# Lasting row tiles, set-up work dealt over the slots, experts that begin three slots later, and fewer scatters between the last blocks

## The chip, the cores and the metric

The kernel runs on one core of a Trainium2 chip. The metric is the device time of one execution in microseconds; less is better. Before the change it is 595.44 us (median of three runs, 592.53 to 595.68).

## What is computed

The input is x, 8 batches of 2496 tokens with 256 features. A filter over each batch's sequence comes first, then a mixture of 8 experts of which each token uses one:

```
X = rfft(x, axis=1);  y = irfft(X * (filt_r + 1j*filt_i), n=2496, axis=1)
x = y.reshape(19968, 256)
logits = x @ w_gate + modality_bias[modality_id]          # 19968 x 8
e = argmax(logits);  gate = max(softmax(logits))
out = gate * (relu(x @ w1[e]) @ w2[e])                    # w1: 256x1024, w2: 1024x256
```

## The kernel before, in words

The transform of length 2496 is written as 48 by 52. Stage 1 multiplies by the 48 part, stage 2 by the 52 part, filters and turns back by 52, stage 3 turns back by 48 and leaves the rows of tokens. Between the stages the data are laid out anew: for batches 0 to 2 on the chip by TensorE transposes (`turned1`, `to_residues`, `to_columns`), for batches 3 to 7 through DRAM (`load_t2`, `load_t4`, on SP's queue). Stage 2 is cut into 12 pieces of two frequencies; `around` runs the forward products of one piece and the inverse ones of the piece ahead of it, with something from another batch between them. One such step, and whatever stands beside it, is a slot here. In the trace the two forward products at L474 open a slot.

Stage 3 has 10 steps of two row groups each. A batch's rows stand in a row tile: 128 partitions, 20 row groups, 130 words each, that is 128 words with the row in 16 bits, one with the token's number (`DW`) and one with its gate. The row tile comes from a pool `yp` of two buffers. At step 0 GpSimd writes the token numbers (L555, the token add) behind the last TensorE mark (`paced`); VectorE and ScalarE write the rows in turn (L599, L597). Each step also transposes rows (L584) and adds up the logits (L589).

After stage 3 a batch is routed: `counting` finds each row's expert and its rank within it, `placing` makes the positions in the experts' bins, `scatter` (L677) writes one row group into the bins in DRAM by an indirect DMA from GpSimd, 20 per batch, and `tabling` finds which expert blocks are full. `pace(k)` issues at most one scatter per call and returns what is left of k, so nested calls issue several.

`Experts` then runs blocks of 256 rows: SP loads the block from the bins (`xs`, L755), TensorE transposes it (L784), multiplies by w1 (L798), by w2 (L811), and two indirect DMAs from GpSimd write the scaled rows to their tokens (L820). One call of `moe.step` is a quarter of a block's products. The weights come during the first stretches by `load_w` on GpSimd's queue, as x does by `load_x`.

The program has five parts, and within them the order on TensorE, ScalarE and VectorE is the order in which the code is written (`manual_schedule`) in the stretches ahead of the merged loop:

- Set-up: the constants of the transform are made, and batch 0's stage 1 runs beside.
- First stretch, `spectrum(0, ...)`: 13 slots with batch 0's stage 2, and more constants at four places between slots; `busy(3)` issues three spare products per slot.
- Second stretch, `both(1, k)`: 15 slots with batch 1's stage 2 and batch 0's stage 3. Third, `both(2, k)`: 15 slots with batch 2's and batch 1's; here batch 0 is routed (`some` takes pieces of it per slot) and scattered.
- Merged loop, n from 0 on: stage 2 and 3 of the later batches, two or three scatters per slot, and 1.5 expert steps per slot. The first blocks of experts start `LAG` slots behind the slot they are given.
- Tail: beyond n = `end` each turn of the loop issues `pace(1)` and one whole block, until batch 7's scatters are out; then blocks alone. Seventy-nine blocks run in all.

Each engine works through its own queue in order. On SP's queue, stage 2's loads of batch 3 stand among the loads of expert blocks; on GpSimd's, token adds stand among scatters, stores of expert rows and loads of x and of weights.

## Time and profile before

| what | value |
|---|---|
| median of three runs | 595.44 us |
| profiled execution, its own time | 595.62 us |
| its span, first to last instruction | 593.4 us |
| mean granted TensorE clock | 0.944 of full speed |
| TensorE products busy | 511.0 us, 86 % |
| VectorE, ScalarE, GpSimd busy | 372.5, 380.4 and 371.5 us |
| scatters (L677) | 160, 164.5 us |
| stores of expert rows (L820) | 158, 161.7 us |

Set-up ends near 25 us; the first stretch runs from 24.8 to about 54, the second from 55 to 79, the third from 81 to about 118, the merged loop begins behind it, the tail at about 397, and blocks run alone from 482.5. Busy time is an average over parts with different limits. The timeline shows each instruction's start, duration and, in brackets, how long its engine had idled and for whom; the windows view gives the engines' busy time in a stretch; the chain of waits goes back from the last instruction. A granted clock near 0.5 is the lower of TensorE's two levels (1.2 GHz of 2.4), and L474's pair then takes 0.63 us in place of 0.38.

### The profile page before, as it was taken

Reading aid. Unit: us, or ns where it says so; the run is one execution under the profiler, and the core shown is the slowest. Engines: PE = TensorE matmul, PEld = TensorE weight load, DVE = VectorE, ACT = ScalarE, POOL = GpSimd, SP = SyncE. Lnnn points to the kernel's source line nnn. Section 1 sums busy time; section 2 is a strip of 40 time slices with the busy share of each in tenths; the row PEclk is TensorE's granted clock in tenths of the full one; section 3 lists DMA queues with packets and bytes.
Section 4 is the critical chain, followed back from the end, with each engine's and each line's share of the span. In section 5 each row is a group of like instructions: output and inputs, shape, how many; then the busy total and the mean of one; then the engine's idle time right before and its main releaser. Section 6 shows DMA issues by size and latency. Waiting matters only on the chain.

```text
span 593.4 us, 16261 instructions
## 1 busy us (share of the span) xinstructions
PE 511.0 (86%) x5115; PEld 461.3 (78%) x5115; DVE 372.5 (63%) x1207; ACT 380.4 (64%) x695; POOL 371.5 (63%) x409
## 2 busy tenths in 40 slices
PE   2678978749988996999898997998999999999990
PEld 2567968638867896988887995986888889999990
DVE  8556978646657677677778785784455365555540
ACT  4677968727847786787786772554656556666660
POOL 8123315737756775676776777777777776555552
PEclk9979998959988999899999997998999999999996
DMA  8999994788498878889758545334433344333220
GB/s 152 177 159 206 211 213 101 175 185 215 127 225 226 226 161 217 227 187 246 225 151 229 158 134 161 95 94 145 140 112 117 118 124 135 109 106 110 93 72 23
DMA packets 69301, 93.29 MB, mean 157 GB/s; under 512 B 11427, under 2 KB 52841, under 8 KB 69059
## 3 DMA queue, kind: packets, MB, share of 16 engines
q0 software_dynamic: 21504, 50.75, 35.0%
q1 hardware_dynamic: 24409, 29.94, 19.7%
q10 hardware_dynamic: 23302, 11.50, 7.5%
q8 instruction: 48, 0.79, 0.6%
q14 instruction: 38, 0.31, 0.2%
HBM read 64.68 MB, written 46.35 MB: 187 GB/s over the span
## 4 chain that ended last, share of the span: by engine, by line
PE 45%; DMA 15%; issue 15%; DVE 10%; POOL 9%; ACT 3%; DVEq 1%; POOLq 0%; SPq 0%; ACTq 0%
PE hps L798 12%; PE ops L811 11%; POOL out_dram L820 7%; DMA out_dram<-osb,meta 5%; DMA t<-b_d 3%; PE ps L474 3%; PE lt L584 3%; PE ps L569 2%; DMA bins_d<-yo,pos_i 2%; PE pz L486 2%; PE pz L487 2%; DMA b_d<-t 2%; PE ps L572 2%; DVE osb L818 2%; PE pT L784 1%
## 5 line engine op out<-in xcount | busy, mean ns | idle before, releaser
L803 ACT ACTIVATE hT<-hps 128x512 f16<-128x512 f32 x316 | 188.3, 598 | 117.2 <-PE hps L798 116.3
L820 POOL DMA_INDIRECT out_dram<-osb,meta x158 | 161.7, 1024 | 80.9 <-DVE osb L818 35.2
L798 PE MATMUL hps<-xT,w 128*128 128x256 f16 x1264 | 201.7, 280 | 5.1 <-DVE xT L785 4.7
L677 POOL DMA_INDIRECT bins_d<-yo,pos_i x160 | 164.5, 1028 | 57.3 <-issue 21.8
L811 PE MATMUL ops<-w2sb,hT 128*128 x1264 | 196.8, 276 | 3.2 <-issue 2.4
L798 PEld LDWEIGHTS <-w 128*128 128x128 f16 x1264 | 147.0, 147 | 12.1 <-DVE xT L785 7.6
L811 PEld LDWEIGHTS <-hT 128*128 128x128 f16 x1264 | 124.9, 99 | 19.6 <-issue 4.2
L818 DVE TENSOR_SCALAR osb<-ops,meta 128x256 f32<-128x256 f32 x158 | 69.5, 477 | 43.1 <-DMA out_dram<-osb,meta 25.7
L776 DVE COPY w<-w1sb 128x2048 f16 x79 | 55.6, 704 | 29.0 <-PE hps L798 27.1
L508 DVE TENSOR_TENSOR p<-xf,g 104x512 f16<-104x512 f16 x96 | 40.5, 421 | 45.3 <-ACT xf L501 45.0
L501 ACT CAST xf<-ps 104x512 f16<-104x512 f32 x96 | 57.3, 597 | 7.8 <-PE ps L474 6.9
L785 DVE COPY xT<-pT 128x512 f16<-128x512 f16 x79 | 33.4, 423 | 41.8 <-PE pT L784 40.8
L523 ACT CAST z<-pz 104x512 f16<-104x512 f32 x72 | 42.9, 596 | 13.1 <-PE pz L487 9.5
L474 PE MATMUL ps<-t,w2m 104*104 104x256 f16 x192 | 39.7, 290 | 7.4 <-DMA t<-b_d 4.5
L219 ACT CAST t<-ps 96x512 f16<-96x512 f32 x52 | 30.2, 581 | 24.0 <-PE ps L215 21.1
L509 DVE TENSOR_TENSOR xf<-xf,g 104x512 f16<-104x512 f16 x96 | 40.5, 422 | 3.0 <-DVE p L508 0.3
L144 POOL DMA_DIRECT2D xt<-in_x_dram x32 | 18.2, 571 | 35.6 <-PE fp L215 13.7
L784 PE MATMUL pT<-ident,xs 128*128 128x128 f16 x316 | 31.5, 223 | 10.1 <-DMA xs<-bins_d 9.5
L486 PE MATMUL pz<-p,a1m 104*104 104x256 f16 x144 | 37.2, 281 | 3.4 <-DVE p L508 1.9
L593 DVE COPY yT<-lt 128x512 f16<-128x512 f16 x80 | 33.4, 418 | 7.1 <-PE lt L589 5.1
L487 PE MATMUL pz<-xf,a2m 104*104 104x256 f16 x144 | 36.6, 279 | 0.0
L584 PE MATMUL lt<-ident,yo 128*128 128x128 f16 x320 | 31.0, 218 | 5.9 <-DVE yo L599 3.2
(206 smaller groups left out, 723.7 us busy)
## 6 DMA issues: line engine op xcount, KB each, us to landing
xs<-bins_d SPq DMA_DIRECT2D x79, 130.0 KB
xt<-in_x_dram POOLq DMA_DIRECT2D x24, 384.0 KB
t<-b_d SPq DMA_DIRECT2D x18, 384.0 KB
t<-b_d SPq DMA_DIRECT2D x15, 416.0 KB
b_d<-z ACTq DMA_DIRECT2D x30, 208.0 KB
b_d<-t ACTq DMA_DIRECT2D x24, 192.0 KB
w1sb<-in_moe_w_dram POOLq DMA_DIRECT2D x16, 256.0 KB
w2sb<-in_moe_w_dram POOLq DMA_DIRECT2D x8, 512.0 KB
```

The source lines that it names most:

```text
L474: mm = nc.tensor.matmul(ps[:KB, i, :], lhsT=w2m[:, s + i, :], rhs=st[g]["t2", s // SCH][:, s % SCH + i, :], start=True, stop=True)
L486: nc.tensor.matmul(pz[:KB, i, :], lhsT=a1m[:, s + i, :], rhs=p1[:, i, :], start=True, stop=False)
L487: nc.tensor.matmul(pz[:KB, i, :], lhsT=a2m[:, s + i, :], rhs=p2[:, i, :], start=False, stop=True)
L501: nc.scalar.copy(xf, ps[:KB])
L584: nc.tensor.transpose(pT[:, i, dc, :], yo[:, ub + i, dc * P:(dc + 1) * P], ident)
L677: ins = nc.gpsimd.indirect_dma_start(out=bins_d[:, :], out_offset=IOA(ap=st[g]["pos"][:rows, t:t + 1], axis=0), in_=st[g]["yw"][:rows, t, ...
L776: cp = nc.vector.tensor_copy(b["w1"].rearrange("p a f -> p (a f)"), w1sb[:, ds(ej, 1)].rearrange("p o a f -> p (o a f)"))
L798: mm = nc.tensor.matmul(hps[:, k, :], lhsT=b["w1"][:, dc, ft:F:FT], rhs=b["xT"][:, dc].rearrange("p i t -> p (i t)"), start=(dc == 0), sto ...
L803: nc.scalar.activation(b["hT"][:, q * FQ:(q + 1) * FQ, :], hps, AF.Relu)
L811: nc.tensor.matmul(b["ops"][:, i, :], lhsT=b["hT"][:, ft, i * P:(i + 1) * P], rhs=w2sb[:, ds(b["ej"], 1), ft, :], start=(ft == 0 and i == ...
L818: nc.vector.tensor_scalar_mul(osb[:, i, :], b["ops"][:, i, :], gate[:, i, :])
L820: ins = nc.gpsimd.indirect_dma_start(out=out[:, :], out_offset=IOA(ap=b["meta"][:, i, 0:1], axis=0), in_=osb[:, i, :], in_offset=None, bou ...
```

## The change

- The two row tiles are made once (`yws`) and batch g uses `yws[g % 2]`, where a pool gave a tile per batch. In set-up the same two tiles hold the raw modality ids and a scratch. The token add stands in `placing`, without `paced`.
- Set-up: eight pieces of batch 0's stage 1 stand before the constants of `w2m` (four before); x loads are issued at other steps; three of the residue turns change engine.
- The four id loads stand in the code behind the first slot. Only the first of them is paced.
- The constants made between slots of the first stretch are dealt one piece per slot, the sine and the exponential behind slot 2. Weight loads are issued from slot 2 on, and in the third stretch too.
- Second and third stretch: stage 3 begins two slots behind the batch's first slot (three before), the first two column turns a slot sooner; each stretch has 14 slots (15 before). In the third stretch, slots without a column turn get three spare products. Routing of batch 0 takes four bare pieces (two before) between `counting` and `placing`, and four pieces per slot in the first three slots, then two (three before).
- Merged loop: the first blocks have slot 1, so their steps begin at n = 3 in place of 0; batch 1 is placed at n = 1; four spare products stand in each of the slots n = 0 to 3. In the tail a turn issues (n - end) modulo 3 scatters by one `pace` call, which is one, one, none, in place of one each.

The order of SP's queue at its start is different from the code's. Before, with the semaphores that each row waits for (`scr` and `mrawc` hold the ids):

```order
L384 DMA g1_68<-g1_68 52x5888 [waits DMASW5_49,DMASW4_49]
L385 DMA g1_68<-g1_68 51x256 [waits DMASW6_49]
L384 DMA g2_69<-g2_69 52x5888 [waits DMASW1_49,DMASW0_49]
L385 DMA g2_69<-g2_69 51x256 [waits DMASW2_49]
L386 DMA scr_105<-in_moe_modality_id_dram 96x8x52
L388 DMA mrawc_106<-in_moe_modality_id_dram 32x8x52
L388 DMA mrawc_106<-in_moe_modality_id_dram 32x8x52 [waits DMAHW0_49]
L388 DMA mrawc_106<-in_moe_modality_id_dram 32x8x52 [waits DMAHW1_49]
L1013 DMA bins_d<-pad_799 128x260 [waits DMAHW2_49,DVE_49]
```

And now (`yo1` and `yo0` are the lasting row tiles):

```order
L964 DMA yo1_106<-in_moe_modality_id_dram 32x8x52 x3
L386 DMA g1_68<-g1_68 52x5888 [waits DMASW5_49,DMASW4_49]
L387 DMA g1_68<-g1_68 51x256 [waits DMASW6_49]
L386 DMA g2_69<-g2_69 52x5888 [waits DMASW1_49,DMASW0_49]
L387 DMA g2_69<-g2_69 51x256 [waits DMAHW0_49,DMASW2_49]
L962 DMA yo0_105<-in_moe_modality_id_dram 96x8x52 [waits DMAHW1_49,PE_49]
L1028 DMA bins_d<-pad_859 128x260 [waits DMAHW2_49,DVE_49]
```

Three of the four id loads moved to the very front, ahead of the moves within the filter tiles `g1` and `g2`; the fourth stands behind these and waits for TensorE. On GpSimd, in set-up, stands now (L632 is the token add, for batch 1; `ident` and `g2` are needed by set-up's TensorE and filter work):

```order
masks.py:197 MEMSET ident_97 128x128
L632 TENSOR_SCALAR yo1_106<-tok_900 128x20 [waits DMAHW4_49,DMAHW3_49,DMAHW2_49]
masks.py:199 AFFINE_SELECT ident_97<-ident_97 128x128 [waits Pool_49]
L323 DMA g2_69<-in_filt_i_dram 26x6144 [waits DMASW0_49]
L324 DMA g2_69<-in_filt_i_dram 26x23x256 [waits DMASW1_49]
```

The token add moved there from the third stretch; before, no instruction stood between the two on `ident`.

GpSimd's queue in the third stretch, from batch 2's last loads of x to batch 1's first scatters, before:

```order
L144 DMA xt_1468<-in_x_dram 96x2048
L144 DMA xt_1535<-in_x_dram 96x2048
L144 DMA xt_1736<-in_x_dram 96x512
L555 TENSOR_SCALAR yo_1741<-tok_815 128x20
L677 DMA bins_d<-yo_1088,pos_i_1709 162048x130 x10
L144 DMA xt_1935<-in_x_dram 96x2048
L677 DMA bins_d<-yo_1088,pos_i_1709 162048x130 x8
L144 DMA xt_2125<-in_x_dram 96x2048
L677 DMA bins_d<-yo_1088,pos_i_1709 162048x130 x2
L144 DMA xt_2163<-in_x_dram 96x2048
L555 TENSOR_SCALAR yo_2354<-tok_815 128x20
L677 DMA bins_d<-yo_1741,pos_i_2278 162048x130 x9
```

And now:

```order
L444 DMA w1sb_465<-in_moe_w1_dram 128x1024
L446 DMA w2sb_466<-in_moe_w2_dram 128x2048
L144 DMA xt_1545<-in_x_dram 96x2048
L144 DMA xt_1753<-in_x_dram 96x512
L675 DMA bins_d<-yo0_105,pos_i_1731 162048x130 x10
L144 DMA xt_1962<-in_x_dram 96x2048
L675 DMA bins_d<-yo0_105,pos_i_1731 162048x130 x8
L144 DMA xt_2160<-in_x_dram 96x2048
L675 DMA bins_d<-yo0_105,pos_i_1731 162048x130 x2
L144 DMA xt_2196<-in_x_dram 96x2048
L632 TENSOR_SCALAR yo0_105<-tok_900 128x20
L675 DMA bins_d<-yo1_106,pos_i_2314 162048x130 x6
```

No token add stands ahead of batch 0's first scatter (L675 is what L677 was); batch 2's, whose row tile is batch 0's, stands right behind batch 0's last scatter.

GpSimd's queue in the tail, where `out` is a block's store and `bins` a scatter, before:

```order
L820 DMA out_0_dram<-osb_8554,meta_8329 19968x256 x2
L677 DMA bins_d<-yo_7522,pos_i_8217 162048x130
L820 DMA out_0_dram<-osb_8649,meta_8424 19968x256 x2
L677 DMA bins_d<-yo_7522,pos_i_8217 162048x130
L820 DMA out_0_dram<-osb_8744,meta_8519 19968x256 x2
L677 DMA bins_d<-yo_7522,pos_i_8217 162048x130
```

And now:

```order
L675 DMA bins_d<-yo1_106,pos_i_8163 162048x130
L818 DMA out_0_dram<-osb_8689,meta_8464 19968x256 x2
L818 DMA out_0_dram<-osb_8783,meta_8559 19968x256 x2
L675 DMA bins_d<-yo1_106,pos_i_8163 162048x130
L818 DMA out_0_dram<-osb_8878,meta_8654 19968x256 x2
L675 DMA bins_d<-yo1_106,pos_i_8163 162048x130
L818 DMA out_0_dram<-osb_8973,meta_8748 19968x256 x2
L818 DMA out_0_dram<-osb_9067,meta_8843 19968x256 x2
```

A scatter stood behind every block's two stores; now every third block has none behind it.

The diff, cut to its core:

```diff
-    yp = ctx.enter_context(tc.tile_pool(name="fy", bufs=2))
+    yp = ctx.enter_context(tc.tile_pool(name="fy", bufs=1))
...
-    scr = yp.tile([P, NY * RW], I32, tag="yo", name="scr")
+    yws = [yp.tile([P, NY, RW], I32, name=f"yo{i}") for i in range(2)]
+    scr = yws[0].rearrange("p t w -> p (t w)")
...
-    mrawc = yp.tile([P, 3, B, 2 * NTT], I32, tag="yo", name="mrawc")
+    mrawc = yws[1].rearrange("p t w -> p (t w)")[:, 0:3 * B * 2 * NTT].rearrange("p (a g w) -> p a g w", a=3, g=B)
...
-        for k in range(4):
+        for k in range(8):
             turned1(0, k)
...
-            for k in range(4, 10) if a == 0 else range(10, len(T1)):
+            for k in range(8, 10) if a == 0 else range(10, len(T1)):
...
-        nc.sync.dma_start(mraw[:KA], mid32)
-        for b in range(3):
-            nc.sync.dma_start(mrawc[KA:P, b], mid32[b * KC:(b + 1) * KC])
...
-            to_residues(0, s0 // SPB, "vs"[s0 // SPB % 2])
-            if 0 < s0 <= (len(TCH) - 1) * SPB:
+            to_residues(0, s0 // SPB, "vsvvsv"[s0 // SPB])
+            if s0 in (0, 2 * SPB, 4 * SPB):
                 load_x(after=True)
...
         if k == 0:
-            yw = yp.tile([P, NY, RW], I32, tag="yo", name="yo")
-            st[g]["yw"] = yw
-            paced(nc.gpsimd.tensor_single_scalar(yw[:, :, DW:DW + 1], tok, g * S, op=ALU.add))
+            st[g]["yw"] = yws[g % 2]
...
         mx, ohT, sc, c = st[g]["route"]
+        nc.gpsimd.tensor_single_scalar(yw[:, :, DW:DW + 1], tok, g * S, op=ALU.add)
         psO = pp.tile([P, 2, E], F32, tag="ps")
...
                 around(g, k, middle)
-                load_w()
-
-        spectrum(0, range(0, 3))
+                if k > 1:
+                    load_w()
+
+        spectrum(0, range(0, 1))
+        paced(nc.sync.dma_start(mraw[:KA], mid32))
+        for b in range(3):
+            nc.sync.dma_start(mrawc[KA:P, b], mid32[b * KC:(b + 1) * KC])
...
-        turns_to_cos(wb48, qb, [KA, N1], rb)
+        ts(rb, qb, RND, RND, ALU.add, ALU.subtract)
+        nc.vector.tensor_sub(qb, qb, rb)
+        spectrum(0, range(2, 3))
+        nc.scalar.activation(wb48, qb, AF.Sin, bias=zbias[:KA, :], scale=TWO_PI)
         nc.scalar.activation(zs, zs, AF.Exp)
...
+        AFT = 2
+
         def both(g, k, beside, on):
...
-                cols = {2: 0, 3: 1, 4: 2, 5: 3, 8: 4, 9: 5, 11: 6}
+                cols = {1: 0, 2: 1, 4: 2, 5: 3, 8: 4, 9: 5, 11: 6}
...
-                if 0 <= k - 3 <= NPY + 1:
-                    stage3(g - 1, k - 3)
+                if 0 <= k - AFT <= NPY + 1:
+                    stage3(g - 1, k - AFT)
+                if g > 1 and k not in cols:
+                    busy(3)
...
             yield from counting(g)
-            yield
-            yield
+            for _ in range(4):
+                yield
             yield from placing(g)
...
-        for k in range(NS // EV + 3):
+        LONG = AFT + NPY + 2
+        for k in range(LONG):
             both(1, k, turned(k), "v")
...
-        n = -(NP + 2)
-        for k in range(NP + 2):
+        n = -LONG
+        for k in range(LONG):
             both(2, k, lambda on: k < NP and input_piece(3, k), "vs"[k % 2])
-            some(3)
+            some(4 if k < 3 else 2)
             pace(pace(2))
+            load_w()
             n += 1
...
     for b in moe.ready:
-        b["slot"] = -LAG
+        b["slot"] = 1
...
-        if n == 0:
+        if n == 1:
             routed(TURNED - 1)
+        if n <= 1 + LAG:
+            busy(4)
...
         else:
-            pace(1)
+            pace((n - end) % 3)
             owed += FT // FQ
```

The rest of the diff deals the VectorE constants between `spectrum` calls, one range of a single slot each, in the order they had.

## Rows read from the trace of the kernel before

**Rows 1.** Windows: us, PE, PEld, DVE, ACT, POOL busy (count), PEclk, DMA share, GB/s.
```profile
54.00:80.00 26.00, 24.66 (x406) 22.92 (x405) 22.60 (x62) 23.20 (x47) 8.23 (x16) 1.00 1.09 213
135.00:397.00 262.00, 239.26 (x2352) 214.57 (x2351) 185.81 (x640) 180.22 (x335) 188.68 (x191) 0.97 0.71 184
397.00:482.50 85.50, 80.39 (x727) 71.59 (x725) 41.31 (x116) 48.06 (x81) 66.00 (x65) 0.98 0.40 125
482.50:578.00 95.50, 95.50 (x920) 90.12 (x918) 50.33 (x127) 61.07 (x103) 54.95 (x56) 1.00 0.34 105
```
**Rows 2.** Timeline, end of set-up: start us, us, engine line op count [idle before <-releaser].
```profile
19.94 2.23 SPq L386 DMA_DIRECT2D scr<-in_moe_modality_id_dram  x1
20.87 0.53 POOL L144 DMA_DIRECT2D xt<-in_x_dram  x1 [6.33 <-PE tt L271]
...
29.11 0.82 PE L254 MATMUL fp<-w1m,xt 96*128 96x96 f16 x8 [3.97 <-DMA xt<-in_x_dram]
```
**Rows 3.** Timeline, first stretch: forward products that open a slot, a table load.
```profile
35.18 0.38 PE L474 MATMUL ps<-t,w2m 104*104 104x256 f16 x2
...
36.96 1.28 ACT L974 ACT_TABLE_LOAD   x1
...
40.55 0.63 PE L474 MATMUL ps<-t,w2m 104*104 104x256 f16 x2
...
51.36 0.38 PE L474 MATMUL ps<-t,w2m 104*104 104x256 f16 x2
```
**Rows 4.** Lines, whole span: count, busy us, mean ns of one, idle before it.
```profile
L501 ACT CAST xf<-ps 104x512 f16<-104x512 f32 x96 | 57.3, 597 | 7.8 <-PE ps L474 6.9 <-DVE ni L704 0.3
```
**Rows 5.** Timeline, third stretch, TensorE: forward products that open a slot.
```profile
82.13 0.38 PE L474 MATMUL ps<-t,w2m 104*104 104x256 f16 x2
...
88.06 0.65 PE L474 MATMUL ps<-t,w2m 104*104 104x256 f16 x2
...
93.96 0.38 PE L474 MATMUL ps<-t,w2m 104*104 104x256 f16 x2
95.95 0.38 PE L474 MATMUL ps<-t,w2m 104*104 104x256 f16 x2
```
**Rows 6.** Timeline, GpSimd: token add, first and last scatter of batch 0.
```profile
93.42 1.13 POOL L555 TENSOR_SCALAR yo<-tok 128x20 int32<-128x20 int32 x1
94.84 1.10 POOL L677 DMA_INDIRECT bins_d<-yo,pos_i  x1 [0.29 <-PE tt L286]
...
120.89 0.91 POOL L677 DMA_INDIRECT bins_d<-yo,pos_i  x1 [0.31 <-issue]
```
**Rows 7.** Timeline, the join: first bin load, forward products of merged slots 1 and 3.
```profile
124.98 0.38 SPq L755 DMA_DIRECT2D xs<-bins_d  x1
...
130.59 0.67 PE L474 MATMUL ps<-t,w2m 104*104 104x256 f16 x2 [0.33 <-DMA t<-b_d]
...
137.08 0.38 PE L474 MATMUL ps<-t,w2m 104*104 104x256 f16 x2
```
**Rows 8.** Chain of waits, merged stretch: scatters waited for (start us, us).
```profile
267.20 4.23 DMA bins_d<-yo,pos_i
...
363.02 2.50 DMA bins_d<-yo,pos_i
```
**Rows 9.** Timeline behind the second of these scatters.
```profile
365.80 0.69 DVE L599 TENSOR_SCALAR yo<-ps 128x512 f16<-128x512 f32 x1 [5.28 <-DMA bins_d<-yo,pos_i]
...
366.55 0.40 PE L584 MATMUL lt<-ident,yo 128*128 128x128 f16 x4 [2.90 <-DVE yo L599]
```
**Rows 10.** Windows of one line each: L784 (twice, PE and PEld), L820, L677 (GpSimd).
```profile
397.40:482.45 85.05, 7.93 (x80) 6.27 (x80) 0.98 0.40 125
482.45:572.33 89.88, 9.26 (x97) 7.34 (x97) 1.00 0.35 108
397.40:482.45 85.05, 40.49 (x40) 0.98 0.40 125
397.40:482.45 85.05, 25.06 (x25) 0.98 0.40 125
```

More of the change, by code (lines that the diff above doesn't have):

```diff
@@ L177, in ts, with turns_to_cos @@
         nc.vector.tensor_scalar(out, in_, scalar1=s1, scalar2=s2, op0=op0, op1=op1)
-    def turns_to_cos(dst, q, shape, r=None):
-        if r is None:
-            r = gen.tile(shape, F32, tag="gen_r", name="r")
+    def turns_to_cos(dst, q, shape):
+        r = gen.tile(shape, F32, tag="gen_r", name="r")
         ts(r, q, RND, RND, ALU.add, ALU.subtract)
@@ L967 @@
         kps = col("kps", lambda t: nc.vector.tensor_scalar_mul(t, kp, 1.0 / N1))
+        spectrum(0, range(1, 2))
         php = col("php", lambda t: nc.vector.tensor_sub(t, bit0, zri))
@@ L980 @@
         nc.vector.tensor_scalar_mul(wbv[:, :, 1], wb48, j1w[:KA])
+        spectrum(0, range(4, 5))
         for b in range(3):
             nc.vector.tensor_copy(wbm[:, 1 + b, KA:P], wbm[:, 0, b * KC:(b + 1) * KC])
-        spectrum(0, range(3, 6))
+        spectrum(0, range(5, 6))
         mv = mraw.rearrange("p g (t two) -> p g t two", two=2)
@@ L986 @@
             nc.vector.tensor_copy(mids[:KA, :, b:NYF:3], mv[:KA, :, b:4 * NYG:4, 0])
+        spectrum(0, range(6, 7))
         nc.vector.tensor_copy(mids[:KA, :, NYF:NY], mv[:KA, :, 4 * NYG:NTT, 0])
         nc.vector.memset(mids[KA:P, :, NYF:NY], 0.0)
+        spectrum(0, range(7, 8))
         for b in range(3):
@@ L991 @@
             nc.vector.tensor_copy(mids[KA:P, :, b:NYF:3], mv[KA:P, :, 3:4 * NYG:4, 0])
-        spectrum(0, range(6, 9))
+        spectrum(0, range(8, 9))
         eio_i = const_pool.tile([P, E], I32)
@@ L1005 @@
         nc.vector.tensor_copy(jio, jio_i)
+        spectrum(0, range(9, 10))
         keep = const_pool.tile([P, E, NY], F32)
@@ L1008 @@
         nc.vector.memset(keep[:, :, 0:1], 0.0)
+        cnt = const_pool.tile([P, E], F32)
+        done = const_pool.tile([P, E], F32)
+        nc.vector.memset(cnt, 0.0)
+        nc.vector.memset(done, 0.0)
+        spectrum(0, range(10, 11))
         pad = const_pool.tile([P, NI, RW], I32)
@@ L1013 @@
         nc.sync.dma_start(bins_d[E * CAP:E * CAP + BLK, :].rearrange("(p i) w -> p i w", i=NI), pad)
-        cnt = const_pool.tile([P, E], F32)
-        done = const_pool.tile([P, E], F32)
-        nc.vector.memset(cnt, 0.0)
-        nc.vector.memset(done, 0.0)
+        spectrum(0, range(11, 12))
         wg = const_pool.tile([P, DC, E], BF16)
@@ L1036 @@
                        base=3, channel_multiplier=NTT)
-        spectrum(0, range(9, NS // EV + 1))
+        spectrum(0, range(12, NS // EV + 1))
         assert ones[0][0] == 2
@@ L1078, in beside @@
             def beside(on):
-                if 2 <= k < NP + 1:
+                if k >= 2:
                     one(on)
```

3 lines of the change are left out of this document (2 added, 1 removed).

## Prediction

> **What bounds the kernel now.** I read the busy time by stretch first [rows 1], then the timeline where TensorE's share drops (end of set-up, first and third stretch, the join), the chain of waits for scatters, and last the tail. The reader is to see three regimes. In the second stretch TensorE is busy 24.66 of 26 us and the DMA share is 1.09, so both are full. In the merged loop (135 to 397) TensorE has 239.26 of 262, with 188.68 us of GpSimd work beside it: TensorE sets the pace, broken by single waits. In the tail to 482.5 the DMA share is only 0.40 and TensorE loses 5 us; behind it TensorE has no gap at all. Time can be saved without taking TensorE work away only in the front, at the join, at the single waits, and in the tail.
>
> The sum is made against the profiled execution, 595.62 us, of which 593.4 us are its span; the 2.2 us around it stay. The median of the runs, 595.44, is 0.2 lower.
>
> **Front, three terms.** A: the first stretch stands 3.97 us for an x load [rows 2]. That load went out at 20.87, released by a transpose group for which its queue had stood 6.33 us; it is issued a step earlier now, and the id loads, one of which took SP 2.23 us to issue in the same microseconds, are gone from there. The wait cannot shrink by more than 3.97. Against it, three id loads now stand at SP's start and GpSimd waits for them in the middle of making `ident`; the trace has no such wait, so I bound it by the 2.23 us of that issue. Range -4.0 to +2.2; I take half the wait, -2.0.
>
> B: the first stretch. A slot needs three ScalarE casts, 597 ns for one [rows 4], the other two taken at 0.5, so 1.6 us. The slot from 35.18 lasts 5.37 [rows 3], because VectorE's constants and the sine and exponential (a table load of 1.28 [rows 3], with the two functions 1.8) stand in one lump. Dealt out, 5.37 becomes 1.6 + 1.8: -2.0. The six slots from 40.55 to 51.36 take 10.81 against 9.6, and the pair at 40.55 takes 0.63 for 0.38, so the lump also cost the clock, which fell to the lower level behind it: -1.2 if it holds. Weight loads that start two slots later are hidden by the second and third stretch, which still have eight and more slots before the first expert; if not, the first block waits at the join, where it now has three slots more. Together -3.2, from 0 to -4.9. The ids come later too and are read from slot 5 on; I add +1 as the other bound.
>
> C: the second stretch has one slot fewer. Fifteen slots in 26 us [rows 1] are 1.7 each, but the slot dropped is one without stage 2 and its products are done elsewhere. I take -0.7, between -1.7 and +1 (the column turn and stage 3 of the same slot now wait for each other).
>
> **D: third stretch.** The slot from 82.13 lasts 5.93 us [rows 5], in which routing's VectorE steps hold up TensorE; the next two take 5.90, at the lower clock (0.65 for the pair), then one takes 1.99 at full clock. With four bare pieces of routing instead of two, VectorE's steps lie over more slots: I take 5.93 to 3.9, -2.0, and the two slots behind at 2.0 each, -1.9. The spare products keep TensorE at work there. Then the token add, 1.13 us and 0.3 around it, is out from ahead of the first scatter [rows 6]: -1.4. The first scatter is 5.3 sooner within the stretch; at the least the 1.4, at the most 7.
>
> The scatters themselves stay: 94.84 to 120.89 for twenty, and the first bin load at 124.98 [rows 7]. These 30.1 us are GpSimd's, issue behind issue, and no part of the change shortens them. So TensorE, which is done with its stretch earlier, waits longer: what is late next is GpSimd.
>
> **E: the join.** The first scatter moves by A + B + C + D = -2.0 - 3.2 - 0.7 - 5.3 = -11.2, and so does the bin load, to 113.8. The load of stage 2's data for batch 3 stands behind two bin loads on SP now, one before: +0.4 (a load's issue is 0.38). The forward products of merged slot 1 come at 130.59 - 11.2 + 0.4 = 119.8. Before, slot 3 followed 6.49 us later with expert steps between; now there are none, and two slots at 2.4 (2.0 as above, and four spare products) make 124.6 against 137.08: -12.5. But the steps left out there are one block, and it runs at the end, where 24 blocks take 89.88 us [rows 10]: +3.7. A to E give -8.8; with every bound at its end, -15 to +5.
>
> How TensorE's fill is judged decides whether that block is dear. In the merged loop products are busy 239.26 of 262 but weight loads 214.57, so some 47 us show no weight load. The Trainium skill (Perfetto Trace Analysis, Identifying the Most-Contended Engine) says product busy time is a bad measure and to go by the weight loads; by it the block could find room and the sum would be 3.7 lower, 575.2. The trace speaks against that here: with the end's weight loads at 90.12 of 95.5, blocks still follow every 3.75 us.
>
> **F: row tiles.** The chain of waits stands on a scatter for 4.23 and 2.50 us in the merged loop [rows 8], where a new row tile waits for all scatters out of the old one; behind one of them VectorE stood 5.28 us and TensorE 2.90 [rows 9]. With lasting tiles a row write waits only for scatters of its own row groups, long landed. I take 2.90 for this, about 1.5 for the other and nothing for the clock: -4.4. The price is the new wait: the token add stands right behind the last scatter out of the same tile and writes a word that this scatter reads, so GpSimd stands until it has landed, 2.5 to 4.2 us by the same two rows, six times. Queued behind it are the next scatters, stores of expert rows and x loads; VectorE waits for the stores through their buffers, TensorE through VectorE. GpSimd has 73 us free of 262 in the loop, so most is absorbed: +2.4 of the 20 in all. Net -2.0; the ends are -6 (all hidden) and +16 (nothing hidden).
>
> **G: tail.** Twenty blocks (80 transposes) take 85.05 us, 4.25 each, against 3.75 where blocks run alone [rows 10]: 10 us too many. GpSimd issues 65 DMAs there, 1.31 us each without rest: three per block are 3.9, above 3.75. With two scatters per three blocks it is 8/3 of 1.31, 3.5 per block, below. The scatters last longer (30 turns of the loop for 20), but none holds a block up. The excess of 10 should go but for the first blocks, where GpSimd is behind by what the merged loop left: -6, from 0 to -10.
>
> **Sum.** 595.6 - 8.8 - 2.0 - 6.0 = 578.8, so 579.
>
> **The rivals.** 1: the front is held by transfers. The DMA share of 1.09 speaks for it: an x load that goes out earlier meets the filter's and weights' loads. Then A, B and C give nothing, 5.9 less, and the time is 585. Against: the waits of rows 2 and 3 are for a release and for VectorE, not for bytes. A rule says the same: the Trainium skill (DMA: Bandwidth & Descriptors, Issuing engines are not separate DMA queues) holds that transfers interleave on the same 16 engines whoever issues them; by that rule the id loads only change place in the crowd. The share above agrees.
>
> 2: the tail stays as it is, because what binds it is not GpSimd's count but its debt: the stores that wait for a landing. G is 0, 585. For: 66.0 of 85.5 us busy is not full; against: 65 times 1.31 is the whole stretch.
>
> 3, slower: the token add blocks GpSimd. Place: the six token adds of the merged loop behind a fresh scatter; price: 2.5 to 4.2 us each, 20 in all, and it decides once the stores held behind it exhaust VectorE's three result buffers, so that TensorE stops. Then F is +18 for -2: 599. Against: slots have stores only every third or so, and GpSimd is free 28 % of the loop.
>
> 4: the change gives more: the block left out at the join hides in the loop, where TensorE has 23 us free (-3.7), and the tail gains all of its 10 (-4): 571. Against: those 23 us are waits, and steps are dealt at 1.5 per slot whether TensorE waits or not.
>
> That it doesn't do what it says holds in one point already: three id loads are in front of the filters and not behind the first slot, which is priced in A.
>
> **How the numbers follow.** Forecast 0.58; rival 1 0.13, rival 2 0.12, both at once (591 to 593, with F at +2 some 595) 0.06; rival 3 0.05; rival 4 0.06. A measurement of this kernel tells 0.5 %, 3 us, from no change. Faster: 0.58 + 0.13 + 0.12 + 0.06 = 0.89; same: 0.06; slower: 0.05. The range, 566 to 593, takes in rivals 1, 2 and 4 with 5 us of the terms' bounds below the last, and leaves rival 3 and the worse part of the double case out. The time of the likeliest case is 579, its own range 573 to 585.
>
> **What would show it.** Right: an x wait near 2 in place of 3.97; no slot above 4 in the first stretch; the first scatter near 83.5 and thirty microseconds from there to the first bin load; a longer TensorE gap at the join, yet merged slot 3 near 124.6; VectorE's row writes without a wait of over 1 us for scatters; token adds that wait 2.5 to 4.2; blocks in the tail every 3.75 to 3.9. Wrong: a first scatter later than 90, which leaves only F and G; tail blocks still at 4.25; VectorE waiting for stores behind each token add.

## The result: slower by 0.8 %

The changed kernel takes 598.99 us (median of 20 runs, 594.51 to 603.33), the kernel before 595.69 (20 runs, 591.85 to 600.68). The ratio is 1.0076, 95 % interval 1.0053 to 1.0100. By the ratio that is 4.5 us; the two medians lie 3.3 us apart. The times given for the runs further down leave out single executions that took over 1.5 % more than the fastest of the same kernel. The profiled execution took 598.22 us with a span of 596.4, 3.0 more than before. Where points of the two profiled executions lie (us from the start):

| point | before | forecast | after |
|---|---|---|---|
| third stretch, first forward products | 80.65 | 74.7 | 79.2 |
| third stretch, last forward products | 110.2 | | 113.8 |
| first scatter | 94.8 | 83.6 | 91.4 |
| first bin load | 125.0 | 113.8 | 125.5 |
| merged slot 1, forward products | 130.6 | 119.8 | 131.6 |
| merged slot 3 | 137.1 | 124.6 | 138.8 |
| last forward products of batch 7 | 348.0 | | 344.3 |
| last scatter of batch 6 | 403.0 | | 404.5 |
| last block begins | 572.3 | | 574.8 |

The front, forecast to be 12.5 us sooner at merged slot 3, was 1.7 later. Behind it the loop, slot 3 to batch 7's last forward products, passed in 205.5 us instead of 210.9, and this was given back before the last block. (In the runs below whose experts start as before it takes 208.5 to 211.6, in those with the late start 204.5 to 209.9. The ranges overlap; by their means, 210.2 and 207.1, some 3 of the 5 us go with the block that is not begun.)

**First stretch.** The second filter's move (SP copies its rows within the tile) went out before the change at

```profile
18.34 0.80 SPq L384 DMA_DIRECT2D g<-g  x1
```

and VectorE had no wait for it. The timeline after, GpSimd, SP and VectorE (start us, us, engine, line, and in brackets the idle time before):

```profile
11.05 1.03 POOL L632 TENSOR_SCALAR yo<-tok 128x20 int32<-128x20 int32 x1 [1.28 <-DMA yo<-in_moe_modality_id_dram]
...
18.17 0.53 POOL L144 DMA_DIRECT2D xt<-in_x_dram  x1 [1.76 <-PE tt L270]
20.50 0.80 SPq L386 DMA_DIRECT2D g<-g  x1
...
21.40 0.71 SPq L387 DMA_DIRECT2D g<-g  x1
...
26.63 0.32 SPq L962 DMA_DIRECT2D yo<-in_moe_modality_id_dram  x1
...
32.99 0.43 DVE L508 TENSOR_TENSOR xf<-xf,g 104x512 f16<-104x512 f16 x1 [7.05 <-DMA g<-g]
```

The x load went out at 18.17 in place of 20.87 [rows 2], as forecast, and TensorE's wait for x there shrank from 3.97 to 1.09 us. But it now goes out ahead of the move of the second filter (20.50, 21.40), where before the move (18.34) went out ahead of the load, and VectorE waited 7.05 us for that move. The clock fell behind the wait:

```profile
29.40:39.40 10.00, 5.93 (x50) 5.22 (x50) 4.03 (x17) 4.39 (x10) 1.10 (x2) 0.50 0.38 61
```

In these 10 us, after, the granted clock is 0.50 and the DMA share 0.38: transfers had little to do there, since the weight loads wait for this stretch's slots. The slots behind it take 1.2 to 2.3 us, none above 4, as forecast; the 12th forward products come at 48.44 against 51.36 [rows 3].

**Second stretch.** From its first forward products to the third stretch's it takes 26.8 us, 25.3 before, with the same TensorE work (24.0 us busy) and the same DMA share (1.09) in both. Among TensorE's waits there after, and not before, is this one (total us, times, longest):

```profile
PE fp L566 <- DVE t L240: 1.9, 3, 0.9
```

Stage 3 (L566) waits for VectorE's copy of a column turn (L240).

**Third stretch.** What was not loaded there came later. ScalarE after:

```profile
96.56 0.58 ACT L218 CAST t<-fp 96x512 f16<-96x512 f32 x1 [5.58 <-DMA b_d<-t]
```

It stands 5.58 us for a write of stage 1 to DRAM (1.2 at most in that stretch before). Two slots from 89.1 to 99.6 take 10.4 us, so the last forward products are 3.6 later though the stretch began 1.4 sooner.

**Join.** GpSimd's first and last scatter, the bin load and the forward products after, to be held against [rows 6, 7]:

```profile
91.39 1.07 POOL L675 DMA_INDIRECT bins_d<-yo,pos_i  x1 [2.98 <-ACT xf L500]
...
119.92 0.91 POOL L675 DMA_INDIRECT bins_d<-yo,pos_i  x1 [0.30 <-issue]
...
125.45 1.22 SPq L753 DMA_DIRECT2D xs<-bins_d  x2
...
131.64 0.67 PE L473 MATMUL ps<-t,w2m 104*104 104x256 f16 x2 [7.90 <-DMA t<-b_d]
135.19 0.64 PE L473 MATMUL ps<-t,w2m 104*104 104x256 f16 x2
138.81 0.38 PE L473 MATMUL ps<-t,w2m 104*104 104x256 f16 x2
140.44 0.38 PE L782 MATMUL pT<-ident,xs 128*128 128x128 f16 x4
```

The chain from first scatter to bin load takes 34.1 us, 3.9 more than before. The two slots from 131.64 to 138.81 take 7.2, with no expert step in them, more than before with them (6.5); the pairs of 0.67 and 0.64 show the lower clock. The first block begins at 140.44; before it began at 127.1.

**Row tiles and GpSimd.** Waits after, to be held against [rows 8, 9]:

```profile
POOL yo L632 <- DMA bins_d<-yo,pos_i: 16.2, 5, 5.5
```

No wait of VectorE or ScalarE for a scatter is left, as forecast. In their place GpSimd stood 16.2 us at five token adds, up to 5.5 at one. The sixth add of the loop stood 4.0 us at 125.4; the profile books that wait under VectorE. Together that is 20.2, the 20 of the prediction. How full GpSimd is, windows of it alone, before and then after:

```profile
135.00:280.00 145.00, 99.96 (x104) 0.96 0.82 204
280.00:397.00 117.00, 88.72 (x88) 0.97 0.57 159
397.00:482.50 85.50, 66.00 (x65) 0.98 0.40 125
```
```profile
135.00:280.00 145.00, 97.93 (x104) 0.98 0.81 206
280.00:397.00 117.00, 87.21 (x87) 0.97 0.55 153
397.00:482.50 85.50, 65.99 (x65) 0.96 0.42 128
```

By busy time GpSimd is at 76 % from 280 to 397. By count it is full: 88 instructions in 117 us are 1.33 each, the same as the 1.32 of the tail (65 in 85.5), where they follow one another without rest. Each stands behind 0.3 us that the profile books as idle, as in

```profile
399.18 0.97 POOL L677 DMA_INDIRECT bins_d<-yo,pos_i  x1 [0.30 <-issue]
400.45 0.97 POOL L677 DMA_INDIRECT bins_d<-yo,pos_i  x1 [0.31 <-issue]
```

(before, tail). Pauses of GpSimd over 0.45 us add up to 20.4 us from 135 to 280 before, but to 3.6 from 280 to 397 and to nothing in the tail. So from 280 GpSimd's queue has next to no room in either kernel, until the tail's backlog is gone, and the 3.6 us by which TensorE is ahead at batch 7's last forward products were lost in front of it. The place is seen in VectorE's waits for stores that still hold its three result buffers, from 394 to 432.5, before and then after (total us, times, longest):

```profile
DVE osb L818 <- DMA out_dram<-osb,meta: 7.7, 2, 5.1
```
```profile
DVE osb L816 <- DMA out_dram<-osb,meta: 11.6, 3, 4.4
```

In these 38.5 us TensorE did 302 products before and 257 after.

**Tail.** Windows of the blocks' transposes after, until GpSimd's backlog is gone and behind it:

```profile
394.55:432.50 37.95, 3.22 (x29) 2.58 (x29) 0.91 0.42 131
432.50:574.80 142.30, 14.64 (x153) 11.59 (x153) 1.00 0.37 112
```

From 432.5 a block takes 3.74 us (142.3 / 38) while scatters still go out, until 504. Before, the slow stretch lasted until 482.5 [rows 10].

### The profile page after: what moved, and what is told of

Read it like the earlier page. It is cut to its first block, busy times and chain, and to the rows that moved or that the text cites. A ratio compares the mean times of both kernels' runs of the same rounds, so it can differ in the third digit from the quotient of the medians.

```text
span 596.4 us, 16317 instructions
## 1 busy us (share of the span) xinstructions
PE 511.1 (86%) x5152; PEld 462.4 (78%) x5152; DVE 376.3 (63%) x1209; ACT 379.7 (64%) x693; POOL 370.0 (62%) x409
## 4 chain that ended last, share of the span: by engine, by line
PE 45%; DMA 11%; issue 10%; DVE 8%; POOL 5%; ACT 2%; DVEq 1%; POOLq 0%; ACTq 0%; SPq 0%
PE hps L796 14%; PE ops L809 14%; POOL out_dram L818 5%; DMA b_d<-z 3%; DMA t<-b_d 3%; DMA out_dram<-osb,meta 3%; PE lt L581 2%; PE ps L566 2%; PE pz L485 2%; PE pz L486 2%; PE ps L473 2%; PE pT L782 2%; PE ps L569 2%; PE ps L214 1%; DMA bins_d<-yo,pos_i 1%
## 5 line engine op out<-in xcount | busy, mean ns | idle before, releaser
L796 PE MATMUL hps<-xT,w 128*128 128x256 f16 x1264 | 199.5, 278 | 7.6 <-DVE xT L783 7.5
L675 POOL DMA_INDIRECT bins_d<-yo,pos_i x160 | 161.8, 1011 | 66.3 <-issue 31.8
L508 DVE TENSOR_TENSOR xf<-xf,g 104x512 f16<-104x512 f16 x96 | 40.4, 421 | 10.1 <-DMA g<-g 7.0
L473 PEld LDWEIGHTS <-w2m 104*104 104x104 f16 x192 | 21.9, 133 | 16.6 <-DMA t<-b_d 13.3
```

What stands on the lines that cost most here:

```text
L473: mm = nc.tensor.matmul(ps[:KB, i, :], lhsT=w2m[:, s + i, :], rhs=st[g]["t2", s // SCH][:, s % SCH + i, :], start=True, stop=True)
L675: ins = nc.gpsimd.indirect_dma_start(out=bins_d[:, :], out_offset=IOA(ap=st[g]["pos"][:rows, t:t + 1], axis=0), in_=st[g]["yw"][:rows, t, ...
L796: mm = nc.tensor.matmul(hps[:, k, :], lhsT=b["w1"][:, dc, ft:F:FT], rhs=b["xT"][:, dc].rearrange("p i t -> p (i t)"), start=(dc == 0), sto ...
```

## The experiments

Each ratio is to runs of the kernel before on the same chip, with its 95 % interval. Where two runs are called not told apart, their intervals overlap.

**e1, weights sooner**, in the changed kernel:

```diff
-                if k > 1:
-                    load_w()
+                load_w()
```

> The changed kernel with weight loads from the first slot of the first stretch on, as before. Theory W (weights that start two slots later still run in the third stretch and hold the writes of stage 1 there: ScalarE stood 5.58 us for such a write at 91 to 97): that wait is gone, the last forward products of the third stretch come near 109 in place of 113.8, and the whole is 3 to 5 us shorter than the changed kernel, ratio to before about 1.001. Rival C (GpSimd's chain of 20 scatters sets the join whatever TensorE does): the wait goes, the first scatter stays near 91.4, the first bin load near 125, and the whole moves by less than 1 us, ratio 1.006 to 1.009.

1.0090 (1.0054 to 1.0127), not told apart from the change. The last forward products of the third stretch came at 108.7, the 5 us of theory W, the 5.58 us wait fell to 1.9 at most, and merged slot 1 was only 1.7 sooner: TensorE stood 10.5 us at the join. In this kernel rival C holds for the time and the first scatter (91.5), though the bin load came 3 us sooner (122.4).

**e2, token add out of set-up:**

```diff
-        nc.gpsimd.tensor_single_scalar(yw[:, :, DW:DW + 1], tok, g * S, op=ALU.add)
+        add = nc.gpsimd.tensor_single_scalar(yw[:, :, DW:DW + 1], tok, g * S, op=ALU.add)
+        if g == 1:
+            paced(add)
```

> The changed kernel with batch 1's token add paced behind TensorE, so that it isn't in set-up; the id loads stay in front. Theory G (GpSimd's wait for the ids delays the second filter's loads by 2.4 us, its move on SP then falls among x loads, VectorE waits 7.05 us for it in the first stretch): the second filter is loaded from 10.5 as before, VectorE's wait is under 2, the third stretch starts 4 to 6 us sooner than 79.2, the whole is 3 to 5 us shorter than the changed kernel, ratio about 1.001. Rival X (x loads crowd the move in any case, since they are issued sooner): the wait stays at 4 us or more and the time changes by less than 1, ratio 1.006 to 1.009.

1.0109 (1.0050 to 1.0167). The second filter was loaded from 10.55, and VectorE waited all the same:

```profile
33.66 0.42 DVE L508 TENSOR_TENSOR xf<-xf,g 104x512 f16<-104x512 f16 x1 [8.67 <-DMA g<-g]
```

Theory G falls: GpSimd's stop in set-up isn't what delays the filter. The move still went out at 19.97, behind the x load at 18.18.

**e3, join as before:**

```diff
-        b["slot"] = 1
+        b["slot"] = -LAG
...
-        if n == 1:
+        if n == 0:
             routed(TURNED - 1)
-        if n <= 1 + LAG:
-            busy(4)
```

> The changed kernel with the join as before: first blocks from merged slot 0 on, batch 1 placed at slot 0, no spare products there. Theory J (the time at the join is idle in any case until the stage 2 data of batch 3 land at 131.6, and a block left out there runs at the end): 3 to 4 us shorter than the changed kernel, ratio about 1.002, the first block near 128, the forward products of slot 3 not over 1 us later than 138.8. Rival S (expert steps in these slots hold stage 2 up by what they take): slot 3 is 3 to 4 us later and the whole the same, ratio 1.006 to 1.009.

1.0021 (0.9986 to 1.0056): 0.55 % or 3.3 us better than the change by the two middle values; the intervals just touch, and d3 below is the clear case. The edit takes back three things at once, the experts' start, batch 1's placing and the spare products. Blocks run while the data come, and merged slot 3 is not later:

```profile
126.56 0.61 PE L782 MATMUL pT<-ident,xs 128*128 128x128 f16 x4 [2.48 <-DMA xs<-bins_d]
130.41 0.59 PE L473 MATMUL ps<-t,w2m 104*104 104x256 f16 x2 [0.86 <-DMA t<-b_d]
...
137.30 0.38 PE L473 MATMUL ps<-t,w2m 104*104 104x256 f16 x2
```

**e4, tail as before:**

```diff
-            pace((n - end) % 3)
+            pace(1)
```

> The changed kernel with one scatter per block in the tail, as before. Theory T (three GpSimd issues of 1.3 us each per block hold a block at 4.0 where it takes 3.75): tail blocks at 4.0 to 4.25 again until the scatters are out, 5 to 8 us longer than the changed kernel, ratio 1.016 to 1.021. Rival Q (GpSimd is full from 280 us on, and its whole queue sets the end of the tail, not the mix): less than 2 us longer, ratio under 1.011.

1.0148 (1.0099 to 1.0198), 0.7 % or 4.3 us worse than the change by the middle values: just short of theory T's span and outside the rival's, but the interval reaches into both and just touches the change's. Its blocks begin 3.96 us apart from 425.6 to 477.1, where the change's stand at 3.74. b1 tells more.

**b1, the tail's pattern alone**, in the kernel before:

```diff
-            pace(1)
+            pace((n - end) % 3)
```

> The kernel before with the changed pattern of scatters in the tail alone (one, one, none per block). Theory T (three issues of 1.3 us per block hold blocks at 4.25, two in three do not): tail blocks at 3.75 once GpSimd has caught up, 3 to 6 us shorter than before, ratio 0.990 to 0.995. Rival Q (GpSimd's whole queue, full since 280, sets the end, and moving scatters behind stores changes nothing): within 1.5 us, ratio 0.998 to 1.002.

0.9937 (0.9906 to 0.9968), -3.7 us. From 421 on its blocks begin 3.7 us apart. Its transposes in a stretch where the kernel before has 33:

```profile
397.40:433.90 36.50, 3.46 (x36) 2.74 (x36) 1.00 0.46 141
```

**b2, lasting tiles alone**, in the kernel before, with the token add in `placing` (for batches 0 and 1 paced, so that it stays out of set-up):

```diff
-            yw = yp.tile([P, NY, RW], I32, tag="yo", name="yo")
-            st[g]["yw"] = yw
-            paced(nc.gpsimd.tensor_single_scalar(yw[:, :, DW:DW + 1], tok, g * S, op=ALU.add))
+            st[g]["yw"] = yws[g % 2]
...
+        add = nc.gpsimd.tensor_single_scalar(yw[:, :, DW:DW + 1], tok, g * S, op=ALU.add)
+        if g < 2:
+            paced(add)
```

> The kernel before with the lasting row tiles and the token add in the placing step, as in the change (for batches 0 and 1 paced, so that neither stands in set-up). Theory F (row writes no longer wait for scatters, and GpSimd's waits at the token adds, some 16 us in all, are mostly absorbed): 1 to 4 us shorter than before, ratio 0.993 to 0.998. Rival B (GpSimd's chain sets the time from 280 us on, so its waits at the token adds push batch 6's last scatter out by 3 us or more from 403): 1 to 4 us longer, ratio 1.002 to 1.007.

1.0061 (1.0032 to 1.0091): the tiles as the change makes them cost 3.6 us.

```profile
POOL yo L634 <- DMA bins_d<-yo,pos_i: 13.2, 5, 4.7
```
```profile
278.61 0.28 POOL L634 TENSOR_SCALAR yo<-tok 128x20 int32<-128x20 int32 x1 [5.51 <-issue]
```

The second line, from the timeline, is the loop's sixth add: the profile names nothing that ended its wait, so the sum in the first lacks it. With it GpSimd stood 18.7 us.

**b3, the same with the token add where it was**, at the start of stage 3:

```diff
-            yw = yp.tile([P, NY, RW], I32, tag="yo", name="yo")
+            yw = yws[g % 2]
             st[g]["yw"] = yw
             paced(nc.gpsimd.tensor_single_scalar(yw[:, :, DW:DW + 1], tok, g * S, op=ALU.add))
```

> The kernel before with the lasting row tiles, the token add where it was, at the start of stage 3. Theory B (what costs is GpSimd standing at the token add behind a fresh scatter): here it stands less than 4 us in all at them, row writes don't wait for scatters, 2 to 5 us shorter than before, ratio 0.992 to 0.997, and shorter than the run with the add in the placing step by 3 us or more. Rival F (those waits are absorbed): both runs with lasting tiles within 1.5 us of each other.

0.9965 (0.9932 to 0.9999), and no GpSimd wait for a scatter at a token add. The two runs differ in the add's place alone, by 0.96 %, 5.7 us. In the profiles GpSimd takes 286.1 us from batch 0's last scatter to batch 6's with the late add and 280.8 with the early one (before 282.1), while TensorE passes the loop in 209.3 and 209.4. (The two profiled executions themselves took 593.70 and 592.65 us; the 5.7 us is that of all runs.) Theory B holds, with a limit: of 18.7 us of waits some 5.3 came through. Up to batch 3's last scatter, at 272, three waits of 8.6 us in all had cost 1.1; behind it three of 10.1 cost 4.3 more. So GpSimd's queue makes up for most of a wait ahead of 272 and for little over half of it behind.

**e7, x loads at the steps of before**, in the changed kernel:

```diff
-            if s0 in (0, 2 * SPB, 4 * SPB):
+            if 0 < s0 <= (len(TCH) - 1) * SPB:
                 load_x(after=True)
```

> The changed kernel with x loads issued at the steps of before. Theory X (the x load issued at 18.2, ahead of the second filter's move on SP at 20, and those behind it crowd that move, which ends at 28 to 33 in place of 24): VectorE's wait for the filter falls from 7 to under 2.5 us and the first stretch ends 4 us sooner, near 44.5; theory C (the join hangs on GpSimd's chain) says that a third to a half of it is left at the first merged slots: 1 to 2.5 us shorter than the changed kernel, ratio 1.003 to 1.006. Rival I (the id load at 26.6, 768 pieces of 208 bytes beside the move's last 512-byte pieces, is what delays it): the wait stays at 5 us or more and the ratio at 1.007 to 1.010.

1.0054 (1.0016 to 1.0092), not told apart from the change. VectorE's wait fell from 7.05 to 4.8, between the two expectations. It began at 25.8, 3 us before the late id load went out (28.79); the x load still went out ahead of the move (19.72 and 20.57).

**c1, mended**: the changed kernel with the join (e3) and the x steps (e7) taken back, and the token add where it was:

```diff
             st[g]["yw"] = yws[g % 2]
+            paced(nc.gpsimd.tensor_single_scalar(st[g]["yw"][:, :, DW:DW + 1], tok, g * S, op=ALU.add))
...
-        nc.gpsimd.tensor_single_scalar(yw[:, :, DW:DW + 1], tok, g * S, op=ALU.add)
```

> The changed kernel with three parts taken back: experts from merged slot 0 on (join as before), the token add at the start of stage 3 as before, x loads at the steps of before. Kept: lasting tiles, the tail's pattern, the dealt constants, stage 3 a slot sooner. Theory (these three are what the change loses: 3.3 us for the join, 4 to 5 for GpSimd's waits, 1.3 for the loads, by the runs so far): 589 to 591 us where before is 594.5, ratio 0.988 to 0.994. Rival (their sizes don't add, because GpSimd's chain of scatters swallows what TensorE gains in front): as good as before with tiles and tail alone or worse, ratio 0.993 to 0.998.

0.9891 (0.9841 to 0.9941), a ratio within the theory's.

**c2, mended, weights from slot 0** (c1 with the edit of e1).

> The mended kernel, with weight loads from the first slot on as before too. Theory W (late weights hold stage 1's writes in the third stretch): last forward products of the third stretch 3 to 5 us sooner than in the mended kernel, the whole 1 to 2.5 us shorter. Rival C (the join hangs on GpSimd's scatters): within 1 us of the mended kernel.

0.9832 (0.9787 to 0.9876); 585.54 us against 588.53, but the intervals overlap. The last forward products of the third stretch came 4.1 sooner, merged slot 3 2.2 sooner.

**c3, before with lasting tiles and the tail's pattern** (the edits of b3 and b1).

> The kernel before with the lasting tiles (token add where it was) and the tail's pattern, and nothing else of the change. Theory (both ease GpSimd's queue at different places, and add): 0.9937 and 0.9965 give 0.990, 588 to 590 us where before is 594.5. Rival (both take out the same backlog, so the second finds nothing): 0.993 to 0.995. Against the mended kernel this run says what the front edits bring: equal if nothing.

0.9899 (0.9862 to 0.9936): the two add up. With 0.9891 for the mended kernel, its front edits had brought nothing yet.

**c4, mended, ids back in set-up:**

```diff
             nc.sync.dma_start(g[N2 + 1:KB, 0, :], g[1:N2, 0, :])
+        nc.sync.dma_start(mraw[:KA], mid32)
+        for b in range(3):
+            nc.sync.dma_start(mrawc[KA:P, b], mid32[b * KC:(b + 1) * KC])
...
-        paced(nc.sync.dma_start(mraw[:KA], mid32))
-        for b in range(3):
-            nc.sync.dma_start(mrawc[KA:P, b], mid32[b * KC:(b + 1) * KC])
```

> The mended kernel with the four id loads back in set-up behind the filter moves. Theory I (an id load of 768 small pieces at 27, beside the last piece of the second filter's move, keeps VectorE waiting 4.8 us for the filter in the run with x loads at the old steps): the wait falls under 2 us, the third stretch starts 3 us sooner, the whole is 0.5 to 2 us shorter than the mended kernel. Rival X (x loads alone crowd the move): the wait stays, the time is within 0.7 us of the mended kernel.

0.9827 (0.9786 to 0.9867), 584.92 us against c1's 588.53, but these intervals overlap too. VectorE's wait for the filter, in the mended kernel and then here:

```profile
DVE xf L508 <- DMA g<-g: 6.4, 1, 6.4
```
```profile
DVE xf L511 <- DMA g<-g: 1.8, 1, 1.8
```

The third stretch begins at 75.6, 2.9 sooner, the first scatter comes at 87.4. But this edit moved something else too: without the three id loads in front the second filter's move went out at 18.99, ahead of the first x load (19.64), where in c1 it went out at 20.08, behind that load (19.66).

**d1, ids back alone**, in the changed kernel with its sooner x loads (the edits of c4 and e2).

> The changed kernel with the four id loads back in set-up behind the filter moves (and batch 1's token add paced, so that it doesn't come with them); x loads stay at the changed steps. Theory I (the id load beside the filter's last pieces is the cause): VectorE's wait for the filter falls from 7 to under 3 us, the third stretch starts 3 to 4 us before 79.2, the whole is 1 to 3 us shorter than the changed kernel, ratio 1.002 to 1.006. Rival X (the sooner x load is enough): the wait stays at 4 us or more, ratio 1.006 to 1.009.

1.0069 (1.0040 to 1.0099); the wait stays at 6.6. So either edit alone, the sooner x loads or the moved id loads, makes VectorE wait; with both taken back 1.8 to 3.0 us are left. Which part of the id edit does it wasn't separated by a run, but the times at which things went out (us) put the order of load and move ahead of theory I:

| run | first x load | second filter's move | late id load | VectorE's wait |
|---|---|---|---|---|
| before | 20.87 | 18.34 | none | none |
| c4 | 19.64 | 18.99 | none | 1.8 |
| d2 | 19.64 | 18.85 | none | 3.0 |
| e7 | 19.72 | 20.57 | 28.79 | 4.8 |
| c1 | 19.66 | 20.08 | 27.11 | 6.4 |
| d1 | 18.17 | 18.49 | none | 6.6 |
| after | 18.17 | 20.50 | 26.63 | 7.05 |
| c2 | 19.64 | 19.77 | 26.11 | 8.1 |

Where the move went out ahead of the first x load the wait is 3.0 or less, where behind it 4.8 or more; so it is in all the runs here (in e1 the profile books the 8.3 us under an x load). The move goes out at 19.8 to 20.8 in every run that has the three id loads in front and at 18.3 to 19.0 in every other.

**d2, mended, ids back and weights from slot 0** (c4 with the edit of e1).

> The mended kernel with ids back in set-up and weights from the first slot, so the dealt constants, the shorter stretches, the lasting tiles and the tail's pattern are what is left of the change. Theory W (late weights hold stage 1's writes in the third stretch): the two gains add, 0.9827 less 0.004 to 0.006, ratio 0.977 to 0.979, 581 to 583 us. Rival C (both free the same wait at the join, set by GpSimd's scatters): 0.981 to 0.984.

0.9786 (0.9741 to 0.9831), 584.21 us against 595.04: the lowest ratio of all, 11 us below before by the medians. The middle value is theory W's, the interval takes in rival C's; the intervals don't tell it from c2 and c4, but from c1 (0.9891). Against the tiles and tail alone (0.9899) the front edits are now worth 1.1 %.

**d3, that kernel with the join of the change** (the edit of e3 the other way round).

> The run before this one with the join as in the change: experts from merged slot 3, batch 1 placed at slot 1, spare products there. Theory J (a block left out at the join is a block more at the end, since the join is idle until data land): 3 to 4 us longer than that run. Rival F (in the changed kernel it cost that only because the front was late; where the data come sooner the slots without expert steps are passed faster): within 1.5 us of it or shorter.

0.9899 (0.9846 to 0.9951): 1.1 % or 6.7 us worse, and these intervals are apart. By the middle values the late start costs more where the front is mended. Windows of 119 to 133 in the run before this one and in this:

```profile
119.00:133.00 14.00, 9.80 (x63) 7.85 (x64) 6.75 (x31) 6.50 (x12) 6.27 (x7) 0.62 0.88 217
```
```profile
119.00:133.00 14.00, 6.26 (x31) 4.86 (x32) 2.72 (x7) 2.83 (x5) 3.29 (x4) 0.50 0.85 207
```

The data land at the same time (forward products of slot 1 at 125.75 and 125.98), TensorE does 31 products instead of 63 meanwhile, and is not faster for it.

## Why the prediction was wrong

The forecast was 579 us and its range 566 to 593; measured were 599.0, and the first scatter came at 91.4, behind the 90 that the prediction had named as a sign of being wrong. Two steps failed above all. The front and the join were to bring merged slot 3 forward by 12.5 us, and it came 1.7 later. And "GpSimd has 73 us free of 262 in the loop, so most is absorbed" was to leave the row tiles a gain of 2.0, and as the change makes them they cost 3.6. Rival 3's 599 is met by luck: its sum has F at +18 and everything else as forecast. (The 575.2 that the prediction gives by weight loads should read 575.1.)

**A, x loads (-2.0).** The load came sooner and its wait shrank by 2.9. What failed is the bound on the other side: I bounded it by a wait on GpSimd (2.2), where it was the filter's move on SP that the sooner load overtook: 7 us in VectorE. The 1.3 us that GpSimd stood in set-up made no difference that e2 shows. I had read SP's queue but not asked which transfer the load would meet. The three id loads in front, priced as a wait of GpSimd, go with a move that goes out 0.8 us or more later; whether the id load behind the first slot adds to the wait stays open.

**B, dealt constants (-3.2) and weights.** The dealing did at least what I said: with little of the filter's wait left (c4) the 12th forward products come at 44.9, 6.5 sooner than before. The step "weight loads that start two slots later are hidden by the second and third stretch" was wrong. The second stretch has a DMA share of 1.09 [rows 1], the row on which I built rival 1; what is put off ahead of a full stretch comes out behind it, in the third, on ScalarE: 5 us there by e1, of which nothing is seen at the end in the changed kernel.

**C and D (-0.7, -5.3).** The second stretch took 26.8 us to the third's first products, 25.3 before. From there to the first scatter it is 12.2 for 14.2, so -2.0 where D had -5.3. In the mended kernel with ids back it is 11.8. C had the wrong sign: the second stretch takes 1.5 more for one slot fewer. It does so in c4, e1 and d2 too (26.8), whenever weights and ids are loaded, so it isn't the transfers; what fits is the bound that C named itself, the column turn and stage 3 of the same slot wait for each other (1.9 us), though no run takes that apart. D was mis-sized: I read a gain for every part of one slow slot.

**E, join (-8.8 with the block).** Slot 3 was 14.2 later than forecast: 7.8 by the first scatter, 3.9 by the chain from it to the bin load, which I took as fixed, 2.4 by the two slots behind, 0.1 between. The 2.4 us slots were taken from full clock; the gap ahead put them at the lower one. The displaced block's 3.7 was right in kind (the join costs 3.3 by e3, 6.7 by d3).

**F, row tiles (-2.0).** The gain was there but small: 1.5 us of the loop in b2 and b3 for 4.4. The 20 us of waits were right too. The step that failed is "GpSimd has 73 us free": that came from busy time, which leaves out the 0.3 us between issues that G of the same prediction counted in its 1.31. Of the 73 us 49 are such gaps; 24 are free, 20 of them ahead of 280. So what was to be absorbed but for 2.4 came through with 5.7 by b2 and b3, +3.6 with the gain in it. This is rival 3's mechanism, to which I gave 0.05, at a smaller price and in another place: its point of decision, stores held back until VectorE lacks result buffers, took 3.2 us in the loop up to 394 and 11.6 in the 38.5 us behind it. The Trainium skill (Perfetto Trace Analysis, Identifying the Most-Contended Engine) says that for GpSimd the share of busy time is a fair measure of how close it is to its limit; here the trace differs, 76 % busy from 280 to 397 in a queue that is full.

**G, tail (-6).** Right in kind. The pattern is worth -3.7 alone (interval -5.6 to -1.9) and 4.3 in the changed kernel. Blocks at 3.74 came from 432; until then GpSimd ran behind and VectorE stood the 11.6 us for stores, which is why it isn't 6.

The forecast had a sum of terms as if each were free to reach the end. By the runs: tail -3.7, tiles +3.6, the join with its late expert start +3.3. With the measured +4.5 (3.3 by the medians) some +1.3 (0.1) remains for the front, by subtraction and not measured, where -12.5 stood. Rival 1 said the front would be held by transfers; it was, though not by bytes in all (the DMA share fell to 0.38) but by an x load that went out ahead of a move. The rule cited there is that transfers interleave whoever issues them (the Trainium skill, DMA: Bandwidth & Descriptors, Issuing engines are not separate DMA queues). The trace agrees: GpSimd's load at 18.17 and SP's move at 20.50 stand in different queues, and VectorE waited 7.05 us.

Not tried: the third stretch's spare products and routing pieces each by itself; the parts of the join each by itself; the three id loads in front without the late one. Why the chain from first scatter to bin load took 4 us more stays open in part. It holds a 1.7 us wait for a row write of ScalarE and a landing that takes 1.4 longer; neither was tested.

## What to carry to other kernels

Judge a queue engine that issues DMAs by its count times the spacing of back-to-back issues, not by busy time: an engine at 76 % can be the bound. A wait put on it is made up for while its queue has room and comes through as the room runs out. Moving a load ahead moves something else behind: list what goes out on the other queues at that time. Loads put off ahead of a stretch whose DMA share is already full come out behind it. Work that runs in a wait for data cost nothing there in these runs, and a block's time or more where it was moved to.

## What the runs showed that I had not expected

An x load that went out 0.1 to 2.7 us ahead of a move on another queue went with a wait of 4.8 to 8.7 us for that move; with the move ahead by 0.6 us or more the wait was 3.0 at most. Between issues of indirect DMAs GpSimd shows 0.30 to 0.31 us of idle time, even with nothing to wait for. And the weights and the ids, of no measurable worth each by itself in the changed kernel (e1, d1), are worth 1 % together in the mended one (c1 to d2).
